# Moving the zero fill of a routed output behind attention, with the last two experts' weights behind the gathers and six output buffers

## The chip, the cores and the metric

One core of a Trainium2 chip. The metric is the device time of one execution in microseconds (us); the kernel before takes 292.96 us, the median of three runs (291.38 to 295.23). The profile was taken in a separate execution, which took 299.41 us and spans 297.6 us from the first to the last instruction. Times read from the profile lie on that longer scale.

## The reference

Two parts follow one another. The first is attention with 32 global and 512 local tokens per head (8 batches, 8 heads, head dimension 64): global queries see all 544 keys; a local query sees the 32 global keys and the local keys within 32 positions of it.

```python
s_g = scale * q_g @ k_all.T                  # k_all = [k_g, k_l]
out_g = sm(s_g) @ v_all
s_ll = where(abs(i - j) <= 32, scale * q_l @ k_l.T, -1e9)
a_l = sm(concat([scale * q_l @ k_g.T, s_ll]))
out_l = a_l @ concat([v_g, v_l])
x = concat([out_g, out_l])                   # rows: 8 * 544 = 4352, columns: 8 * 64 = 512
```

The second is a mixture of 8 experts over the rows of x. Each row goes to the expert with its largest logit; an expert keeps the 80 rows with the largest gate weight; all other rows of the result are zero.

```python
expert_idx = argmax(x @ w_gate); gate_w = softmax(x @ w_gate)[expert_idx]
out = zeros((4352, 512))
for e in range(8):
    tok = rows with expert_idx == e, the 80 with the largest gate_w
    out[tok] = gate_w[tok] * (relu(x[tok] @ w1[e]) @ w2[e])   # w1: 512 x 1024, w2: 1024 x 512
```

So of 4352 rows at most 640 are written with values, and the whole result, 8.9 MB, must first be filled with zeros.

## The kernel before, in words

**Attention** is a loop of 16 steps, q = 0 to 15: batch q // 2, and the heads 0 to 3 or 4 to 7. A step is written out by hand as a sequence of pieces, and pieces of the next steps are laid between those of the current one, so that the order of the program is the order of work on each engine. The pieces that matter here: `load_qk(q + 4)` and `load_v(q + 2)` put the loads of later steps on SyncE's queue; `G_all` (L380) starts the sums of a step on PE with the global keys and needs `vg`; `shift_v` (L209, L210) makes the second, shifted copy of the values on GpSimd and needs the values' loads; `H_chunk` (L393) adds the banded part for a head and divides; `C_chunk` (L436) casts the result on GpSimd into `xb`, of which there are two buffers, one for each of two batches.

**Gating.** `La`, `Lb1`, `Lm`, `Lb2`, `Lb3`, `Lc` compute a batch's logits, the largest one and the gate weights; `Ld` writes the batch's rows to the scratch tensor `x_scr` in HBM by six transfers on SyncE's queue (L541 to L546). They run a batch behind attention. `best` and `rounds` search the 80 largest weights of each expert by repeated 8-fold maxima on DVE, in small pieces (`some`) between the attention's; the last ten rounds, on `fin`, follow when all batches are in (L802).

**Zeros.** `zeros(n)` issues the next n of 17 writes of 512 KB from a zero tile `zt` to the output, on SyncE's queue (L614). The list `NZ` says how many go out in each step: none in q 0 and 1, one in each of q 2 to 13, two in q 14 and three in q 15. `zeros(17)` after the loop (L780) issues what is left.

**Weights.** `load_w(e, parts)` loads an expert's two matrices in four transfers of 512 KB (bf16 on the chip, float32 in HBM; the cast is done by the transfer), on GpSimd's queue: parts 0 and 1 are w1 (L597), parts 2 and 3 are w2 (L601). Experts 0 to 2 (NRES = 3) are loaded one part in each of q 0 to 11. Expert 3 follows in q 12 and 13, expert 4 in q 14 and 15, the first half of expert 5 in q 15, into buffers that attention no longer needs. The rest of expert 5 and all of expert 6 are issued right after attention (L791). Then come two constants, `tri` and `iota1`, also through GpSimd's queue, because they are cast to bf16 (L792, L793).

**Routing.** From the last rounds come the thresholds; `keep` marks the kept rows, `excl` (L822) and the product with `tri` (L825) number them, four one-hot compares with `iota1` (L836) and 40 small products turn the numbers into row indices `idx` (L847). Eight gathers on GpSimd (L851) fetch the experts' rows from `x_scr`. Right behind them stand the four transfers of expert 7 (L854).

**Experts.** A loop over e: `fx(e + 1)` transposes the next expert's rows and copies them (`fxT`, DVE, L864); `fh(e)` multiplies by w1 with a relu on ACT (L872, L874); `fy(e - 1)` multiplies by w2 (L879), scales into `y` on DVE (L882) and scatters y to the output from GpSimd (L885). `y` has three buffers, taken in turn. `warm(n)` issues n products that nobody reads, so that PE does not fall idle.

What sets the order around the change: three queues with an order of their own. SyncE issues loads, zeros and x_scr in program order; GpSimd issues weights, constants, gathers and scatters in program order between its own computing; and DVE runs the rounds, the copies `fxT` and the scaling `y` in program order.

Of the kernel before, what the change touches and what calls it, by code (L numbers as in the profile page):

```python
# [10 lines left out]
FP32 = mybir.dt.float32  # L11
FP16 = mybir.dt.float16
BF16 = mybir.dt.bfloat16
# [10 lines left out]
NRES = 3  # L24
# [62 lines left out]
def kernel(  # L87
# [18 lines left out]
    E = moe_w_gate.shape[1]  # L106
    DF = moe_w1.shape[1]
# [4 lines left out]
    cap = int(moe_capacity)  # L112
# [17 lines left out]
    def psS(shape, dt, name):  # L130
        return ps.tile(shape, dt, tag="S", bufs=2, name=name)
# [4 lines left out]
    def const(name, dt, shape=None):  # L136
        t = cpool.tile(list(shape or c[name].shape), dt, name=name + ("_b" if dt == BF16 else ""))
        eng = nc.sync if dt == mybir.dt.from_np(c[name].dtype) else nc.gpsimd
        eng.dma_start(out=t, in_=cd[name].ap())
        return t  # L140
# [14 lines left out]
    def load_qk(q):  # L155
        b, qd = divmod(q, 2)
        for t, src in ((0, q_l), (1, k_l)):
            hs = src[b, 4 * qd:4 * qd + 4].rearrange("(g a) (p i) d -> (a p) g (i d)", a=2, i=8)
            nc.sync.dma_start(out=qkb[q % 2][:, t].rearrange("p g i d -> p g (i d)"), in_=hs)

    def regroup(q, t):
        if t == 0:
            qkr[q] = lpool.tile([P, 2, 8, 2, D], FP16, tag="qkr", name=f"qkr_{q}")
        nc.scalar.copy(out=qkr[q][:, t].rearrange("p i g d -> p g i d"), in_=qkb[q % 2][:, t])  # L164
# [134 lines left out]
    def kg_copy(q):  # L299
        b, qd = divmod(q, 2)  # L300
        nc.gpsimd.tensor_copy(out=qkT[q % 2][:, :, 512:544], in_=kgp[:, b, 2 * qd:2 * qd + 2, :])

    def kO_copy(q):

        for a in range(2):
            nc.gpsimd.tensor_copy(  # L306
                out=kO[q % 2][:, a],
                in_=qkT[q % 2][:, a, 576:1088].rearrange("x (u w y) -> x u w y", w=2, y=64)[:, :, ::-1, :])
# [285 lines left out]
    def load_w(e, parts):  # L594
        for k in parts:
            if k < 2:
                nc.gpsimd.dma_start(out=w1sb[e][:, 2 * k:2 * k + 2],  # L597
                                    in_=moe_w1[e, 256 * k:256 * k + 256].rearrange("(c p) f -> p c f", p=P))
            else:
                k -= 2  # L600
                nc.gpsimd.dma_start(out=w2sb[e][:, 4 * k:4 * k + 4],  # L601
                                    in_=moe_w2[e, 512 * k:512 * k + 512].rearrange("(p c) f -> p c f", c=4))
# [2 lines left out]
    QB = 1  # L605

    NS = [[1, 1, 1]] * 11 + [[1, 2, 2]] * 4 + [[2, 2, 0]]
    NZ = [0, 0, 1, 1, 1, 1, 1, 1, 1, 1, 1, 1, 1, 1, 2, 3]
    nz = [0]

    def zeros(n):
        for _ in range(n):
            if nz[0] < 17:
                nc.sync.dma_start(out=out_z[nz[0]], in_=zt[:])  # L614
                nz[0] += 1
# [7 lines left out]
    def warm(n):  # L623

        w_ps = psS([P, 512], FP32, "w_ps")
        for _ in range(n):
            nc.tensor.matmul(out=w_ps[:], lhsT=onesb[:], rhs=w1sb[0][:, 0, 0:512], start=True, stop=True)  # L627
# [23 lines left out]
    for q in range(NQ):  # L651
        b, qd = divmod(q, 2)
        first = q == 0
        if 0 < q and q + 4 < NQ:
            load_qk(q + 4)
        if q + 2 < NQ:
            load_v(q + 2)
        zeros(NZ[q])
        if first:
            for t in range(2):  # L660
                regroup(1, t)
            load_qk(3)
        if late is not None:
            Lb3(late)
        G_chunk(q)
        if not first and q + 2 < NQ:
            kg_copy(q + 2)
        G_all(q)
        H_chunk(q, 0)
        Q_chunk(q)  # L670
        if first:
            T_chunk(1, 0)
        elif q + 2 < NQ:
            T_chunk(q + 2, 0)
        if late is not None and q == NQ - 1:
            Lc(late)
            Ld(late)
        if first:
            T_chunk(1, 1)
            kO_copy(1)  # L680
        elif q + 1 < NQ:
            L_fill(q + 1, 0)
            mask(q + 1, 0)
        if pend is not None:
            La(pend)
        if not first and q + 3 < NQ:
            regroup(q + 3, 0)
        if q + 1 < NQ:
            shift_v(q + 1)
        some(NS[q][0])  # L690
        H_chunk(q, 2)
        if pend is not None:
            Lb1(pend)
        some(NS[q][1])
        if first:
            L_fill(1, 0)
            mask(1, 0)
            for t in range(2):
                regroup(2, t)
        else:  # L700
            if q + 1 < NQ:
                L_fill(q + 1, 1)
            if q + 2 < NQ:
                T_chunk(q + 2, 1)
                kO_copy(q + 2)
        H_chunk(q, 1)
        if not first and q + 1 < NQ:
            mask(q + 1, 1)
        if first:
            L_fill(1, 1)  # L710
            mask(1, 1)
            T_chunk(2, 0)
        if late is not None and q < NQ - 1:
            Lc(late)
            Ld(late)
        if q + 1 < NQ:
            G_fill(q + 1)
            Q_fill(q + 1, 0)
        if not first and q + 3 < NQ:
            regroup(q + 3, 1)  # L720
        H_chunk(q, 3)
        if first:
            T_chunk(2, 1)
            kO_copy(2)
        X_chunk(q, 0)
        if q + 1 < NQ:
            Q_fill(q + 1, 1)
        C_chunk(q)
        X_chunk(q, 1)
        if pend is not None:  # L730
            Lm(pend)
            Lb2(pend)
        if q in (1, 3):
            setup_globals(4, 8, 2 - q // 2 - 1)
        if first:
            for t in range(2):
                regroup(3, t)
            load_qk(4)
        some(NS[q][2])
        late = pend  # L740
        pend = b if qd == 1 else None
        st.pop(q)

        if q < 4 * NRES:
            e, k = divmod(q, 4)
            if k == 0:
                w_tiles(e, wpool)
            load_w(e, (k,))
        if q == 12:

            flat = [qkb[i][:].rearrange("p t g i d -> p (t g i d)").bitcast(BF16) for i in range(2)]
            flat += [vb[i][:].rearrange("p s h d -> p (s h d)")[:, 0:2048].bitcast(BF16) for i in (1, 2, 0)]
            for i, f in enumerate(flat):
                if i % 2 == 0:
                    w1sb[NRES + i // 2] = f.rearrange("p (c f) -> p c f", c=4)
                else:
                    w2sb[NRES + i // 2] = f.rearrange("p (c f) -> p c f", c=8)
            load_w(NRES, (0, 1))
        if q == 13:
            load_w(NRES, (2, 3))  # L760
        if q == 14:
            load_w(NRES + 1, (0, 1))
        if q == NQ - 1:
            load_w(NRES + 1, (2, 3))
            load_w(NRES + 2, (0, 1))
    warm(2)
    La(pend)
    warm(3)
# [17 lines left out]
    for e in range(NRES + 2, E):  # L786
        if e > NRES + 2:
            w1sb[e] = w2pool.tile([P, 4, FF], BF16, name=f"w1sb{e}")
        w2sb[e] = w2pool.tile([P, 8, DF], BF16, name=f"w2sb{e}")
        if e < E - 1:  # L790
            load_w(e, (2, 3) if e == NRES + 2 else (0, 1, 2, 3))  # L791
    tri = const("tri", BF16)  # L792
    iota1 = const("iota1", BF16)  # L793
    rpool = ctx.enter_context(tc.tile_pool(name="route", bufs=1, reuse_waits="tile"))
    xg = [rpool.tile([cap, XW], FP32, name=f"xg{e}") for e in range(E)]
    for e in range(E):
# [53 lines left out]
    for e in range(E):  # L850
        nc.gpsimd.indirect_dma_start(out=xg[e][:], out_offset=None, in_=x_dram.ap(),  # L851
                                     in_offset=bass.IndirectOffsetOnAxis(ap=idx[:, e:e + 1], axis=0),
                                     bounds_check=N - 1, oob_is_err=False)
    load_w(E - 1, (0, 1, 2, 3))  # L854
    warm(16)
    xTs, hTs = {}, {}

# [18 lines left out]
    def fy(e):  # L876
        y_ps = psS([cap, DF], FP32, f"y_ps{e}")
        for cc in range(8):
            nc.tensor.matmul(out=y_ps[:], lhsT=hTs[e][:, cc, :], rhs=w2sb[e][:, cc, :],  # L879
                             start=(cc == 0), stop=(cc == 7))  # L880
        y = rpool.tile([cap, DF], FP32, tag="y", bufs=3, name=f"y{e}")
        nc.vector.tensor_scalar(out=y[:], in0=y_ps[:], scalar1=xg[e][:, XW - 1:XW], scalar2=None,  # L882
                                op0=ALU.mult)

        sc = nc.gpsimd.indirect_dma_start(out=out,  # L885
                                     out_offset=bass.IndirectOffsetOnAxis(ap=idx[:, e:e + 1], axis=0),
                                     in_=y[:], in_offset=None, bounds_check=N - 1, oob_is_err=False)
        tc.declare_no_dep(sc.ins, group="scatters", reason="disjoint rows")
        tc.add_to_no_dep_group("scatters", sc.ins)
# [45 lines left out]
```

The softmax here doesn't subtract the row's maximum and nothing guards it: scores larger than these inputs give would overflow.

## Time and profile before

| | |
|---|---|
| device time, median of 3 | 292.96 us |
| span of the profile | 297.6 us |
| busy: PE, DVE, ACT, POOL | 80%, 53%, 46%, 52% |
| DMA: SyncE's queue, GpSimd's queue | 41.44 MB, 18.80 MB; 52.6% and 34.4% of 16 engines |
| 17 zero writes | 512 KB each, 5.1 us from issue to landing (median) |
| first G_all of q 4, of q 15 | 65.15 us, 199.76 us |
| idx ready, first gather issued | 253.3 us, 254.20 us |
| first transfer of expert 7 issued | 264.08 us |

How to read it: PE is TensorE, PEld its weight loads, POOL is GpSimd, SP is SyncE, DVE and ACT are VectorE and ScalarE. A line of the chain of work that ended last gives the start, the duration and what it was, with the line of the code; "DMA a<-b" in it is the time from the issue of a transfer to its landing. A line of the waits gives who waited for whom, the total in us, how often, and the longest. In a table of stretches, the columns are the stretch, its length, then the busy time of PE, PEld, DVE, ACT and POOL with the number of instructions, PE's granted clock, the mean busy share of the 16 DMA engines (it can pass 1, as packets overlap), and the GB/s they moved.

### The profile page before, as it was taken

What the parts mean: (1) busy time and instruction counts of PE and PEld (TensorE: products, weight loads), DVE (VectorE), ACT (ScalarE), POOL (GpSimd) and SP (SyncE); (2) the same over time, 40 slices, a digit from 0 to 9 for tenths busy, and PEclk for the clock granted to TensorE, in tenths of its full rate; (3) what the DMA queues carried; (4) which work ended last, traced back from release to release, by engine and by line L of the source; (5) the groups of instructions that cost most, each with busy time, mean ns of one, the idle gap of its engine ahead of it and who ended that gap; (6) DMA issues with size and microseconds to landing.
All of it is one profiled execution on the core that took longest, in us unless ns stands there. A gap on an engine that the chain in (4) does not pass through costs nothing.

```text
span 297.6 us, 9689 instructions
## 1 busy us (share of the span) xinstructions
PE 238.7 (80%) x4013; PEld 170.2 (57%) x4017; DVE 157.1 (53%) x521; ACT 135.7 (46%) x225; POOL 155.6 (52%) x220
## 2 busy tenths in 40 slices
PE   1377899999969999975999898994969548999490
PEld 1265676876747776854686776673524215477350
DVE  4652344752831466783476469869668836121221
ACT  3376895786772876753469286450100000033010
POOL 2235677683828759642873868764442200682212
PEclk9999999999996999998699799999669975699776
DMA  7899799699999999996999988999999990149411
GB/s 207 217 266 221 258 274 224 127 291 200 239 228 297 245 229 275 201 215 181 263 241 249 280 187 162 262 211 291 219 230 226 223 183 0 46 89 212 120 44 44
DMA packets 70892, 60.86 MB, mean 204 GB/s; under 512 B 49216, under 2 KB 53568, under 8 KB 70848
## 3 DMA queue, kind: packets, MB, share of 16 engines
q1 hardware_dynamic: 63008, 41.44, 52.6%
q0 software_dynamic: 7840, 18.80, 34.4%
q8 instruction: 31, 0.51, 0.7%
q14 instruction: 13, 0.11, 0.1%
HBM read 62.36 MB, written 14.70 MB: 259 GB/s over the span
## 4 chain that ended last, share of the span: by engine, by line
PE 40%; DMA 26%; issue 9%; ACT 8%; DVE 7%; SPq 4%; POOL 4%; POOLq 0%; ACTq 0%; DVEq 0%
PE o_ps L393 7%; DMA tri_b<-ctri 6%; DMA vb<-in_moe_w_dram 5%; PE o_ps L380 5%; DMA x_scr<-xb 4%; PE T_ps L294 4%; DMA vg<-in_v_g_dram 4%; PE og L409 3%; PE x_ps L425 3%; ACT qkT L297 3%; DMA out_dram<-y,idx 3%; DMA vb<-in_q_g_dram 3%; ACT eL L352 2%; PE lt_ps L447 2%; PE l_ps L347 2%
## 5 line engine op out<-in xcount | busy, mean ns | idle before, releaser
L297 ACT COPY qkT<-T_ps 128x1024 f16<-128x1024 f16 x32 | 32.5, 1020 | 46.4 <-PE T_ps L294 42.8
L360 POOL TENSOR_TENSOR eL<-eL,band 128x512 f32<-128x512 f32 x30 | 38.0, 1266 | 20.6 <-ACT eL L352 18.5
L393 PE MATMUL o_ps<-vb,eL 128*64 128x65 f32 x1024 | 45.6, 234 | 0.1
L352 ACT ACTIVATE eL<-l_ps 128x512 f32<-128x512 f32 x64 | 35.0, 603 | 17.6 <-PE l_ps L347 17.6
L398 DVE RECIPROCAL rec<-o_ps 128x4 f32<-128x4 f32 x64 | 11.5, 179 | 58.8 <-PE o_ps L393 58.7
L393 PEld LDWEIGHTS o_ps<-vb,eL 128*64 128x64 f32 x1024 | 36.6, 142 | 10.1 <-issue 5.9
L164 ACT CAST qkr<-qkb 128x1024 f16<-128x1024 f32 x32 | 33.8, 1066 | 3.1 <-DMA qkb<-in_q_l_dram 3.1
L874 ACT ACTIVATE fhT<-h_ps 128x320 bf16<-128x320 f32 x16 | 6.9, 437 | 61.8 <-PE h_ps L872 60.9
L294 PE MATMUL T_ps<-ident,qkr 128*128 128x128 f16 x256 | 22.0, 234 | 9.8 <-ACT qkr L164 8.8
L627 PE MATMUL w_ps<-w1sb,onesb 128*128 128x512 bf16 x87 | 28.7, 488 | 0.5 <-DVE dthr L814 0.2
L399 DVE TENSOR_TENSOR xn<-o_ps,rec 128x256 f32<-128x256 f32 x64 | 27.2, 425 | 3.2
L209 POOL COPY vb<-vb 64x1040 f32<-64x1040 f32 x16 | 16.7, 1042 | 21.4 <-DMA vb<-in_v_l_dram 11.9
L380 PE MATMUL o_ps<-vg,eG 32*128 32x65 f32 x512 | 22.4, 303 | 6.8 <-DMA vg<-in_v_g_dram 6.8
L306 POOL COPY kO<-qkT 128x512 f16<-128x512 f16 x32 | 18.6, 609 | 16.4 <-ACT qkT L297 15.9
L425 PE MATMUL x_ps<-misc,xn 128*128 128x128 f32 x128 | 21.6, 295 | 5.0 <-DVE rec L398 3.3
L380 PEld LDWEIGHTS o_ps<-vg,eG 32*128 32x128 f32 x512 | 20.0, 211 | 9.5 <-DMA vg<-in_v_g_dram 7.6
L294 PEld LDWEIGHTS <-qkr 128*128 128x128 f16 x256 | 16.1, 104 | 12.8 <-ACT qkr L164 9.2
L436 POOL CAST xb<-xn 128x1024 bf16<-128x1024 f32 x16 | 16.6, 1035 | 10.8 <-DMA x_scr<-xb 5.6
L851 POOL DMA_INDIRECT xg<-x_scr,idx x8 | 7.8, 969 | 23.5 <-DVE idx L847 21.4
L627 PEld LDWEIGHTS <-onesb 128*128 128x128 bf16 x91 | 10.3, 119 | 15.8 <-issue 9.9
L425 PEld LDWEIGHTS x_ps<-misc,xn 128*128 128x128 f32 x128 | 14.1, 145 | 7.8 <-issue 3.4
L882 DVE TENSOR_SCALAR y<-y_ps,xg 80x512 f32<-80x512 f32 x8 | 6.0, 746 | 22.8 <-PE y_ps L879 14.6
(142 smaller groups left out, 450.1 us busy)
## 6 DMA issues: line engine op xcount, KB each, us to landing
out_dram<-zt SPq DMA_DIRECT2D x17, 512.0 KB, 5.1
qkb<-in_q_l_dram SPq DMA_DIRECT2D x16, 512.0 KB, 6.5
qkb<-in_k_l_dram SPq DMA_DIRECT2D x16, 512.0 KB, 4.8
vb<-in_v_l_dram SPq DMA_DIRECT2D x48, 128.0 KB, 5.3
w2sb<-in_moe_w_dram POOLq DMA_DIRECT2D x12, 512.0 KB, 9.0
w1sb<-in_moe_w_dram POOLq DMA_DIRECT2D x10, 512.0 KB, 8.4
x_scr<-xb SPq DMA_DIRECT2D x8, 514.0 KB
vb<-in_moe_w_dram POOLq DMA_DIRECT2D x6, 512.0 KB, 15.0
```

What stands on the lines that cost most here:

```text
L164: nc.scalar.copy(out=qkr[q][:, t].rearrange("p i g d -> p g i d"), in_=qkb[q % 2][:, t])
L209: nc.gpsimd.tensor_copy(out=v[0:64, 5:9], in_=v[0:64, 1:5])
L294: nc.tensor.transpose(out=T_ps[:, i].rearrange("x a p -> x (a p)"), in_=qkr[q][:, t, i].rearrange("p g d -> p (g d)"), identity=ident16[:, :])
L297: nc.scalar.copy(out=dst, in_=T_ps[:].rearrange("x i a p -> x a p i"))
L306: nc.gpsimd.tensor_copy(out=kO[q % 2][:, a], in_=qkT[q % 2][:, a, 576:1088].rearrange("x (u w y) -> x u w y", w=2, y=64)[:, :, ::-1, :])
L352: nc.scalar.activation(out=eL[:], in_=l_ps[hh][:], func=AF.Exp, scale=scale)
L360: eng.tensor_tensor(out=eL[:], in0=eL[:], in1=band[:].rearrange("p t i -> p (t i)"), op=ALU.mult)
L380: nc.tensor.matmul(out=s["o"][h][:, u, :], lhsT=s["eG"][32 * r:32 * r + 32, 128 * u:128 * u + 128], rhs=vg[b % 2][32 * r:32 * r + 32, qd, ...
L393: nc.tensor.matmul(out=o[64 * odd:64 * odd + 64, u, :], lhsT=s["eL"][h][:, 64 * t:64 * t + 64], rhs=v[:, 5 * odd + u, h, :], start=False, ...
L399: nc.vector.tensor_tensor(out=s["xn"][:, :, 64 * h:64 * h + 64], in0=o[:, :, 0:64], in1=rec[:].unsqueeze(2).to_broadcast([P, 4, 64]), op=A ...
L425: nc.tensor.transpose(out=x_ps[:, 128 * u:128 * u + 128], in_=s["xn"][:, u, 128 * j:128 * j + 128], identity=identf[:, :])
L627: nc.tensor.matmul(out=w_ps[:], lhsT=onesb[:], rhs=w1sb[0][:, 0, 0:512], start=True, stop=True)
```

## The change

No zeros are written during attention. The first four of the 17 writes stand right behind the attention loop, the other 13 where the remainder stood before, behind `Ld` of the last batch; all of them must have landed before the first scatter. The two constants are loaded in q 14 instead of behind all the weights. The four transfers of expert 6 move from before the routing to behind the gathers, ahead of those of expert 7. `y` gets six buffers. The aim is to keep the zeros' traffic away from the loads that attention waits for, to let the routing wait for no transfer, and to let the results wait for no scatter.

```diff
@@ -605,7 +605,6 @@
     NS = [[1, 1, 1]] * 11 + [[1, 2, 2]] * 4 + [[2, 2, 0]]
-    NZ = [0, 0, 1, 1, 1, 1, 1, 1, 1, 1, 1, 1, 1, 1, 2, 3]
     nz = [0]
@@ -655,7 +654,6 @@
             load_v(q + 2)
-        zeros(NZ[q])
         if first:
@@ -759,10 +757,13 @@
         if q == 14:
+            tri = const("tri", BF16)
+            iota1 = const("iota1", BF16)
             load_w(NRES + 1, (0, 1))
         if q == NQ - 1:
             load_w(NRES + 1, (2, 3))
             load_w(NRES + 2, (0, 1))
+    zeros(4)
     warm(2)
@@ -787,10 +788,7 @@
         w2sb[e] = w2pool.tile([P, 8, DF], BF16, name=f"w2sb{e}")
-        if e < E - 1:
-            load_w(e, (2, 3) if e == NRES + 2 else (0, 1, 2, 3))
-    tri = const("tri", BF16)
-    iota1 = const("iota1", BF16)
+    load_w(NRES + 2, (2, 3))
@@ -851,7 +849,8 @@
-    load_w(E - 1, (0, 1, 2, 3))
+    for e in range(NRES + 3, E):
+        load_w(e, (0, 1, 2, 3))
     warm(16)
@@ -878,7 +877,7 @@
-        y = rpool.tile([cap, DF], FP32, tag="y", bufs=3, name=f"y{e}")
+        y = rpool.tile([cap, DF], FP32, tag="y", bufs=6, name=f"y{e}")
```

## The prediction

> **What bounds the kernel now.** I read the page's slices first, then stretches of the span, the chain that ended last, the waits, and the queues of SyncE and GpSimd around the end. The page's slices (7.44 us each):
>
> ```profile
> PEclk9999999999996999998699799999669975699776
> DMA  7899799699999999996999988999999990149411
> GB/s 207 217 266 221 258 274 224 127 291 200 239 228 297 245 229 275 201 215 181 263 241 249 280 187 162 262 211 291 219 230 226 223 183 0 46 89 212 120 44 44
> ```
>
> The DMA engines are full from slice 2 to slice 32 (15 to 246 us), idle in 33 and 34, full for one slice, then nearly idle. So there are two regimes, and a hole between them. The same in stretches (columns: PE, PEld, DVE, ACT, POOL busy, granted clock, DMA share, GB/s):
>
> ```profile
> 60.00:200.00 140.00, 125.18 (x2495) 95.76 (x2498) 81.75 (x277) 87.29 (x147) 92.46 (x120) 0.94 1.01 235
> 211.00:246.00 35.00, 24.41 (x105) 10.41 (x106) 24.09 (x80) 0.82 (x2) 8.87 (x22) 0.79 1.07 219
> 246.00:265.00 19.00, 18.06 (x176) 10.94 (x178) 6.96 (x13) 1.78 (x5) 8.67 (x10) 0.67 0.15 34
> 265.00:278.00 13.00, 11.40 (x157) 8.07 (x155) 2.12 (x5) 3.36 (x8) 4.61 (x6) 1.00 1.00 199
> ```
>
> In attention PE is also busy, 125 of 140 us. Which one sets the pace shows in the chain, at the start of each q (G_all, L380):
>
> ```profile
> 103.69 1.05 PE o_ps L380 x32
> 113.17 1.16 PE o_ps L380 x31
> 124.93 1.05 PE o_ps L380 x32
> ...
> 133.61 5.70 DMA vg<-in_v_g_dram
> 139.35 2.55 PE o_ps L380 x32
> ```
>
> Undisturbed, two q take 124.93 - 103.69 = 21.2 us. But q 10 starts 14.4 us after q 9, behind a late vg load, and then runs its first stages at half speed (2.55 for 1.05 us). From q 4 (65.15) to q 15 (199.76) eleven q take 134.6 us; at 21.2 a pair they would take 116.8. So late loads cost attention up to 17.8 us.
>
> After attention the chain ends in these waits:
>
> ```profile
> 227.21 19.00 DMA tri_b<-ctri
> 246.25 0.45 PE pos_ps L825
> ...
> 268.47 1.74 PE y_ps L879 x8
> ...
> 271.26 8.55 DMA out_dram<-y,idx
> ```
>
> tri is a 32 KB constant, but queued behind all of e=5 and e=6: it lands 19 us after issue, and the waits charge PE pos_ps 4.4 us to it. Later y3, the first to reuse one of three buffers, waits for a scatter (8.2 us in the waits) that lies in the software queue behind the weights of e=7; behind y3 on DVE stands fxT of e=6, for which PE waits:
>
> ```profile
> DVE y L882 <- DMA out_dram<-y,idx: 8.2, 1, 8.2
> ...
> POOL xb L436 <- DMA x_scr<-xb: 5.6, 1, 5.6
> ...
> PE pos_ps L825 <- DMA tri_b<-ctri: 4.4, 1, 4.4
> ```
>
> **What the Trainium skill says.** "DMA: Bandwidth & Descriptors", section "Issuing engines are not separate DMA queues": what SyncE and GpSimd issue runs on the same 16 DMA engines and interleaves. Agreed: in 60 to 200 us SyncE's queue holds 68.9% and GpSimd's 31.2% of them, together full. So moved zeros only change whom they compete with. Same page, "Queues, rings and completion order": each DMA engine takes turns between queue rows, and starts a ring's descriptors in order. Agreed: tri and the scatter wait behind weights of their own queue, 19 and about 9 us. "TensorE: Matmul & The Clock Gate", "Part 1: The HAM clock gate": an idle window of about 3.4 us halves the clock until some 3.4 us of work. Agreed: after 3.4 us of idle time, 2.55 instead of 1.05 us above, and a granted clock of 0.70 in 140 to 150 us.
>
> **The change, part by part.**
>
> *Zeros out of attention.* The DMA table for 60 to 200 us lists 13 of the 17 writes of 512 KB (0.524 MB); the other four go out by 206. In 200 to 206 us, where they are 90% of the traffic, the queues moved 285 GB/s: 0.524/285 is 1.84 us each. Thirteen make 24 us of full DMA, more than the 17.8 us that loads cost the chain. So attention should become PE's own. I don't take all of it: the loads lag already when q 4 begins (its q and k loads are issued at 74.6, it began at 65.15), before more than two zeros; small disturbances of PE remain. I take two thirds, 12 us; bounds 4 and 17. The 5.6 us wait of xb (GpSimd) is likely to go too, since x_scr of batch 5 (issued 191.00) no longer stands among zeros; it is inside these 12.
>
> *Zeros after attention.* Issue on SyncE takes 0.43 us each. Queued behind the first four there is only Ld(7), six writes to x_scr, which the gathers need some 25 us later: no cost. The other 13 go behind Ld(7): that ends at 227.7 now, so about 216. From about 197 the DMA must move 17 zeros (31 us), e=4's second half and e=5 (six of 0.524 MB at the 196 GB/s of 266 to 276 us: 16 us), and x_scr of two batches (about 3.7 us): 51 us, done at about 248. The scatters wait for the zeros, but are issued after that. No cost, with no slack to the weights behind the gathers.
>
> *tri and iota1 at q 14.* Two issues of 0.53 us on GpSimd. Behind them are e=4's first loads and rv, xgb and xb of q 15; GpSimd sat idle 5.6 us there: nothing. Removed: 4.4 us on the chain, since excl was ready at 242.3 and PE was free.
>
> *DVE's rounds and the rest up to idx* hang on no transfer: from the attention's end they keep their length. So idx, now at 253.3, comes at 253.3 - 12 - 4.4 = 236.9.
>
> *Weights of e=6 and e=7 behind the gathers.* Now e=7 alone is issued at 264.08, 10.8 us after idx (eight gathers of 1.26 us each). Now two experts: eight issues, twice 2.74 us, with the scatters queued behind them on GpSimd; y0 to y5 have buffers, so nobody waits. Data start 1.4 us after issue and run at 196 GB/s, 2.1 MB an expert: 10.7 us each. So e=6 is there at 236.9 + 10.8 + 1.4 + 10.7 = 259.8, and e=7 at 270.5. The experts run 3.03 us apart; e=0 came 6.5 us after idx, so e=6 is due at 236.9 + 6.5 + 18.2 = 261.6: not late. e=7 is due at 264.6; its w1, the first half, is there at 265.2, but fy(7) waits for w2 until 270.5.
>
> *Six buffers.* They take out the 8.2 us wait and the half-speed stage behind it (h 2.29 for 1.31, y 3.55 for 1.90 us). y6 waits for the scatter of y0, which lands just after e=7's weights: under 2 us, beside fy(7). Behind it on DVE stands only y7.
>
> *Sum.* From 270.5: 1 us for the landing to be seen, fy(7) 1.9 to 3.6 us (2.7), and from its last matmul to the end as now 297.6 - 290.7 = 6.9. End at 281.1, against 297.6. The tail from idx keeps its length (44.2, now 44.3): the second expert on the path costs 10.7 and gives back the buffer wait. The gain is 12 + 4.4 us. The profiled execution was a long one; the median is 292.96. 292.96 x 281.1/297.6 is 276.7. Since the median run has likely fewer of the late loads that the change removes, I add 2.3: **279 us**.
>
> **The rivals.**
>
> *Zeros collide with the weights (no change).* For it: 248 us is the very moment at which e=6 starts. If a zero costs 2.4 us (at 219 GB/s, the rate of 211 to 246), 13 from 216 take 31 us, and some 8 more for what the weights of e=5 take: 255. Gathers then land late and e=6, e=7 lose half the engines for about 7 us: with attention giving only 8, the end is near 281.1 + 4 + 4 + 3 = 292, by the ratio 288. Against it: the 285 GB/s seen.
>
> *Attention is not freed (slower).* The lag is SyncE's: its loads, in order, wait for room. If zeros filled gaps only, idx comes at 249, zeros end near 227.7 + 31 + 16 = 275, and take half the engines from e=6 and e=7 for 14 us, 7 lost: e=7 at 289.6. Six scatters of 0.164 MB behind it, 0.84 us each, hold y6 and y7 (5 us), and PE is cold (3 us): 289.6 + 1 + 3.6 + 6.9 + 5 = 306, by the ratio 301. Against it: DMA at 1.01 through 140 us leaves no gaps.
>
> *Everything fits (faster still).* 17 us from attention, fy(7) warm: 275 in the profile, 271.
>
> **How the numbers follow.** Forecast 0.60, everything fits 0.17, collision 0.15, not freed 0.08. Faster by over 2% means under 287.1: the first two, 0.77; within 2% 0.15; slower 0.08. The range runs from 271 to 292: the low end is the best case, the high end takes in the collision with the 4 us bound for attention.
>
> **What would show it.** No zero before the last q; eleven q from 4 to 15 in about 122 us instead of 134.6; no wait on tri; idx near 237; DMA full from 197 to about 248, and again from 250 to 270; y waits on no scatter before y6; y7 behind w2 of e=7. It is wrong if vg or v still comes late at q 6, 10 or 14, or if zeros are still moving when e=6's weights start.

## The result and the profile after

The changed kernel takes 279.16 us (median of 4, 278.71 to 283.38) beside 294.1 us for the kernel before (now four runs): a ratio of 0.952, 95% interval 0.941 to 0.962. The forecast was 279. The first profile of the kernel before shows an execution 5 us longer than its median, so the two spans (297.6 and 277.2 us) differ by more than the times.

The page's slices of the changed kernel, now 6.93 us each:

```profile
PEclk9999999999999999999999999999968967859998
DMA  7998799896979999899899989969999999379981
GB/s 214 236 261 237 210 292 300 174 246 147 257 125 248 201 241 260 173 218 261 165 270 214 235 150 162 198 118 138 273 266 248 273 420 418 103 123 214 216 226 48
```

PE's clock no longer drops anywhere in attention, and the DMA engines now have some free moments there (a share of 0.95 for 1.01); the zeros show as two slices at 420 GB/s (222 to 236 us). In stretches, columns as before:

```profile
60.00:200.00 140.00, 125.92 (x2662) 94.93 (x2661) 95.04 (x329) 89.47 (x151) 99.83 (x133) 1.00 0.95 203
211.00:246.00 35.00, 27.13 (x185) 13.26 (x184) 19.38 (x42) 0.88 (x3) 9.72 (x11) 0.82 0.86 273
246.00:265.00 19.00, 19.00 (x238) 13.20 (x236) 4.88 (x10) 5.02 (x12) 7.91 (x11) 0.88 1.08 208
```

The hole in DMA at 246 to 265 us is filled (1.08 for 0.15): there e=6 and e=7 are loaded. Starts of some q in the chain that ended last:

```profile
86.86 1.05 PE o_ps L380 x32
...
108.04 1.05 PE o_ps L380 x32
119.70 1.05 PE o_ps L380 x32
...
142.64 1.05 PE o_ps L380 x32
```

These are q 6, 8, 9 and 11. Two q take 21.2 us before q 8, and none of these stages runs at half speed. One load is still late: v before q 10, for which GpSimd waits 3.7 us, so that q 9 to q 11 take 22.9 us. From q 4 to q 15 PE now takes 120.3 us, before 134.7. In PE's own timeline the two stages, and the first product with tri, are

```profile
65.24 1.12 PE L380 MATMUL o_ps<-vg,eG 32*128 32x65 f32 x32
...
185.55 1.12 PE L380 MATMUL o_ps<-vg,eG 32*128 32x65 f32 x32
...
226.20 0.47 PE L823 MATMUL pos_ps<-keepx,tri_b 128*128 128x320 bf16 x1
```

The last line has no wait in brackets: the routing no longer waits for tri. idx and the first gather, from the timelines of DVE and GpSimd, of the changed kernel:

```profile
233.10 0.16 DVE L845 TENSOR_TENSOR idx<-idf,inv_ps 80x8 uint32<-80x8 f32 x1
...
234.14 1.04 POOL L849 DMA_INDIRECT xg<-x_scr,idx  x1 [25.84 <-DMA out_dram<-zt]
```

The bracket names a zero as releaser, but it is idx: the gather comes 0.88 us after idx ends, as it did before (253.32 and 254.20). The chain that ended last is led astray in the same way here.

### The profile page after: what moved, and what is told of

The parts are those of the page before. It is cut to its first block, busy times and chain, and to the rows that moved or that the text cites. A ratio compares the mean times of both kernels' runs of the same rounds, so it can differ in the third digit from the quotient of the medians.

```text
span 277.2 us, 9695 instructions
## 1 busy us (share of the span) xinstructions
PE 228.6 (82%) x4017; PEld 161.9 (58%) x4017; DVE 158.6 (57%) x521; ACT 135.7 (49%) x225; POOL 155.0 (56%) x220
## 4 chain that ended last, share of the span: by engine, by line
PE 44%; DMA 17%; ACT 11%; issue 10%; DVE 7%; POOL 6%; SPq 1%; POOLq 1%; ACTq 0%; DVEq 0%
PE o_ps L393 7%; DMA out_dram<-zt 6%; PE x_ps L425 5%; PE T_ps L294 5%; DMA x_scr<-xb 5%; ACT qkT L297 4%; PE o_ps L380 4%; PE y_ps L878 4%; ACT eL L352 3%; PE h_ps L871 3%; PE og L409 3%; DMA vb<-in_v_l_dram 2%; PE lt_ps L447 2%; PE lg L457 2%; PE l_ps L347 2%
## 5 line engine op out<-in xcount | busy, mean ns | idle before, releaser
L393 PE MATMUL o_ps<-vb,eL 128*64 128x65 f32 x1024 | 44.7, 231 | 0.2 <-POOL vb L210 0.2
L352 ACT ACTIVATE eL<-l_ps 128x512 f32<-128x512 f32 x64 | 35.0, 604 | 17.8 <-PE l_ps L347 17.8
L393 PEld LDWEIGHTS o_ps<-vb,eL 128*64 128x64 f32 x1024 | 35.9, 140 | 10.2 <-issue 6.1
L306 POOL COPY kO<-qkT 128x512 f16<-128x512 f16 x32 | 18.6, 608 | 16.5 <-ACT qkT L297 16.0
L626 PE MATMUL w_ps<-w1sb,onesb 128*128 128x512 bf16 x91 | 27.4, 463 | 0.0
L425 PE MATMUL x_ps<-misc,xn 128*128 128x128 f32 x128 | 20.7, 286 | 5.9 <-DVE rec L398 3.4
L209 POOL COPY vb<-vb 64x1040 f32<-64x1040 f32 x16 | 16.7, 1042 | 9.8 <-DMA vb<-in_v_l_dram 9.8
L436 POOL CAST xb<-xn 128x1024 bf16<-128x1024 f32 x16 | 16.5, 1034 | 6.0 <-DVE xn L399 6.0
L380 PE MATMUL o_ps<-vg,eG 32*128 32x65 f32 x512 | 18.8, 285 | 0.0
L425 PEld LDWEIGHTS x_ps<-misc,xn 128*128 128x128 f32 x128 | 13.4, 140 | 8.7 <-issue 3.5
L380 PEld LDWEIGHTS o_ps<-vg,eG 32*128 32x128 f32 x512 | 16.5, 194 | 2.5 <-issue 2.2
L626 PEld LDWEIGHTS <-onesb 128*128 128x128 bf16 x91 | 9.7, 112 | 14.1 <-issue 7.4
L210 POOL COPY vb<-vb 64x1040 f32<-64x1040 f32 x16 | 16.8, 1052 | 0.9
```

The lines of the kernel that those rows point to most:

```text
L210: nc.gpsimd.tensor_copy(out=v[64:128, 5:9], in_=v[64:128, 0:4])
L306: nc.gpsimd.tensor_copy(out=kO[q % 2][:, a], in_=qkT[q % 2][:, a, 576:1088].rearrange("x (u w y) -> x u w y", w=2, y=64)[:, :, ::-1, :])
L352: nc.scalar.activation(out=eL[:], in_=l_ps[hh][:], func=AF.Exp, scale=scale)
L380: nc.tensor.matmul(out=s["o"][h][:, u, :], lhsT=s["eG"][32 * r:32 * r + 32, 128 * u:128 * u + 128], rhs=vg[b % 2][32 * r:32 * r + 32, qd, ...
L393: nc.tensor.matmul(out=o[64 * odd:64 * odd + 64, u, :], lhsT=s["eL"][h][:, 64 * t:64 * t + 64], rhs=v[:, 5 * odd + u, h, :], start=False, ...
L425: nc.tensor.transpose(out=x_ps[:, 128 * u:128 * u + 128], in_=s["xn"][:, u, 128 * j:128 * j + 128], identity=identf[:, :])
```

## The experiments

The edits are printed in short form, without the lines that only follow from them. "The tail" is the stretch from the end of idx to the end of the profile; its length and that of the stretch before it are taken from the profile of each run.

Zeros and the rest, taken apart. **First, the rest alone:** the zeros go back into attention.

```diff
+    NZ = [0, 0, 1, 1, 1, 1, 1, 1, 1, 1, 1, 1, 1, 1, 2, 3]
 ...
+        zeros(NZ[q])
 ...
     zeros(4)                       # stays; finds none left to write
```

> The changed kernel with the zeros back inside attention, one write a step as before; constants, weights and six buffers as changed. My theory: most of the gain is attention that no longer waits for loads, so q 4 to q 15 takes again some 132 to 135 us instead of 120.3, and the time is 289 to 293 us (the kernel before less the wait for tri, 4.4 us, less a little of the tail). Rival: the gain is in the tail (no wait for tri, no wait of y for a scatter), and attention's late loads come from chance; then the time stays within 3 us of the changed kernel, 277 to 282.

Measured: 295.17 us, ratio 1.008 [1.003, 1.014]. q 4 to q 15 took 132.2 us. The rest alone brings nothing; so neither of the two expectations for the time held, though the one for attention did. In its profile (a span of 292.2 us) idx comes at 248.2 us, 5.1 us earlier than in the first profile of the kernel before: 2.5 us less from q 4 to q 15, and 4.3 us less from q 15 to idx, where the wait for tri is gone, but q 4 starts 1.6 us later. The tail keeps 44 us. The medians don't show these 5 us. As that first profile lies 5 us above the median of its kernel, what the end of this wait is worth by itself stays open.

**The zeros alone:** the kernel before with `NZ` removed and `zeros(4)` behind the loop.

```diff
-    NZ = [0, 0, 1, 1, 1, 1, 1, 1, 1, 1, 1, 1, 1, 1, 2, 3]
 ...
-        zeros(NZ[q])
 ...
+    zeros(4)                       # behind the loop; the rest as in the kernel before
```

> The kernel before with nothing changed but the zeros, which stand behind attention. My theory: attention gains its 14 us, but all weights up to e=6 and the zeros now compete before the routing: 26 us of zeros and 27 us of weights from about 195 us end near 248, tri is again the last in its queue and lands near 243 to 248, so idx is as late as before (250 to 255) and the tail keeps its wait for a scatter: 288 to 295 us. Rival: the parts add up, and this one alone brings some 12 us: 280 to 283.

Measured: 289.52 us, ratio 0.982 [0.975, 0.989]. Attention took 119.2 us from q 4 to q 15, 15 us less; only a third arrives at the end. The waits and the chain of this kernel:

```profile
PE pos_ps L824 <- DMA tri_b<-ctri: 10.3, 1, 10.3
```

```profile
212.82 25.43 DMA tri_b<-ctri
238.29 0.45 PE pos_ps L824
```

tri, last in its queue, lands 25 us after its issue. That is 8 us earlier than in the kernel before (238.25 for 246.21), but attention ends 14 us earlier, so the wait grew from 4.4 to 10.3 us, and idx comes at 245.4 us, not between 250 and 255 as expected. So the parts don't add up (0.982 x 1.008 is 0.990, not 0.952): attention's gain passes through only if routing has no transfer to wait for. Less this wait the 289.5 us would be about 279.2, the time of the changed kernel.

**Which part frees tri?** The changed kernel with the constants loaded where they were, behind e=5:

```diff
-            tri, iota1 = const(...)      # in q 14
+    tri, iota1 = const(...)              # behind load_w(NRES + 2, (2, 3))
```

> The changed kernel with tri and iota1 loaded where they were, behind the weights of e=5. Theory one, as predicted: loading them early takes 4.4 us out of the chain, so this gives some of it back, 281 to 284 us. Theory two, after the changed kernel's trace: with e=6 moved behind the gathers GpSimd's queue is empty at about 220 us, and tri is wanted only at 226.5, so the place of tri is worth nothing by itself: 278 to 280.

Measured: 279.5 us, ratio 0.952 [0.944, 0.959], as theory two had it: the place of tri is worth nothing here. With e=6 behind the gathers tri lands in time even as the last in its queue; PE waits for it no more than in the changed kernel.

**e=6 back before the routing**, constants early:

```diff
     load_w(NRES + 2, (2, 3))
+    load_w(NRES + 3, (0, 1, 2, 3))       # and only e=7 behind the gathers
```

> The changed kernel with the weights of e=6 issued before the routing, as they were; only e=7 follows the gathers. My theory: these 10.7 us of DMA fit ahead of the routing, because the zeros moved at 1.3 us each, not 1.84; zeros end near 247 instead of 238 and slow the gathers and the first part of e=7, but e=7 lands some 5 to 8 us earlier (near 260), and then PE is the last: 4 to 7 us less, 272 to 275. Rival: the zeros and gathers get in each other's way, e=7 lands as late as now: 279 to 284.

Measured: 277.01 us, ratio 0.937 [0.926, 0.948]. At least as good as the changed kernel; the intervals overlap. The time lies between the two expectations. The tail is 40.7 us long, for 43.9 in the changed kernel, although the first rows are used only 6.5 us after their gather is issued. Nobody waits for tri here either: either move frees it, both are not needed.

**Three buffers for y** in the changed kernel:

```diff
-        y = rpool.tile(..., tag="y", bufs=6)
+        y = rpool.tile(..., tag="y", bufs=3)
```

> The changed kernel with three buffers for y. My theory: y3, due at 259.6 us, must wait for the scatter of y0, which lies behind the weights of e=7 and lands near 268; the copy for e=6 stands behind y3 on DVE, PE stops after fy(3) or fy(4) for some 6 us and runs e=6 and e=7 afterwards partly at half speed: 6 to 9 us more, 285 to 288. Rival: the tail is bound by the landing of e=7's weights in any case, and the buffers are worth 1 to 2 us: 280 to 281.

Measured: 289.68 us, ratio 0.985 [0.978, 0.993]; more than expected. The wait, which was 8.2 us in the kernel before, when one expert stood ahead of the scatters, is now for two:

```profile
DVE y L881 <- DMA out_dram<-y,idx: 19.3, 1, 19.3
```

**Eight buffers:** the same line with `bufs=8`.

> The changed kernel with eight buffers for y, so that no y waits for a scatter. My theory: y6 no longer waits for the scatter of y0 (2.8 us in the changed kernel, 9.6 us where PE was quicker), but y7 waits for fy(7), which waits for e=7's w2, so the end moves by 1 us or less: 277.5 to 279.5. Rival: the wait of y6 is what sets the end; 2 us less or more.

Measured: 282.47 us, ratio 0.952 [0.940, 0.963], the ratio of six buffers; the tail has 44.3 us. y6 now waits for fy(6), which stands on PE behind the h of e=7 and so waits for e=7's w1. The scatter ahead of y6 set nothing that shows.

**No zeros at all:** `if nz[0] < 0` in `zeros`, so nothing is written but the scatters.

> The changed kernel with no zero written at all (so rows that no expert keeps stay unwritten). What do the zeros still cost where they stand now? My theory: idx comes from DVE's rounds, the first gather follows idx by 0.9 us as before, and the zeros are through at about 238 us; only the gathers land sooner (4.2 us after issue now, 2.6 without): first gather at 233 to 234.5 us, time 277 to 279.5. Rival: the zeros hold the gathers, as the waits name them for 25.8 us before the first gather; then the gathers go out earlier and the time falls by 4 us or more, below 275.

Measured: 281.93 us (277.74 to 285.34), ratio 0.961 [0.949, 0.974]: above what was expected, and no faster than with zeros. The same two lines as above:

```profile
231.78 0.16 DVE L845 TENSOR_TENSOR idx<-idf,inv_ps 80x8 uint32<-80x8 f32 x1
...
232.81 1.04 POOL L849 DMA_INDIRECT xg<-x_scr,idx  x1 [26.18 <-DVE idx L845]
```

0.87 us again, and now idx is named: the zeros did not hold back the issue of the gathers. Where they stand in the changed kernel, the zeros cost nothing that these runs show.

**What makes zeros hurt?** The kernel of zeros_in_attention, with the zeros issued from another engine: first ScalarE, then GpSimd.

```diff
-                nc.sync.dma_start(out=out_z[nz[0]], in_=zt[:])
+                nc.scalar.dma_start(out=out_z[nz[0]], in_=zt[:])    # second: nc.gpsimd
```

> As zeros_in_attention (zeros inside attention, the rest as changed), but the zeros are issued from ScalarE's queue instead of SyncE's, so no load stands behind a zero in a queue's order. What makes zeros hurt attention? My theory: the time of the 16 DMA engines, which both queues share; then q 4 to q 15 still takes 128 to 135 us and the time stays at 289 to 297. Rival: the order in SyncE's queue, where each load waits for the zero ahead of it; then attention takes 120 to 123 us and the time is 279 to 284.

Measured: 292.69 us; in its profile 135.4 us from q 4 to q 15. But 9.7 of these are one wait, in which ScalarE itself stood still until it had issued a zero (88.79 us), while the profile names the landing of a load of values, so this run decides nothing.

> As zeros_in_attention, but the zeros are issued from GpSimd's queue, where they share a ring with the weights, which nobody in attention waits for. From ScalarE's queue the test was spoilt: one issue held ScalarE itself for 9.7 us. Theory one: what loads lose to zeros is total time of the 16 DMA engines; then it does not matter which queue the zeros take, q 4 to q 15 takes 128 to 135 us, and the time is 289 to 296. Theory two: loads lose only what stands in their own queue ahead of them, and a share of the engines against other queues that does not grow when those have more work; then attention takes 120 to 124 us, the weights come later instead, and the time is 276 to 283.

Measured: 299.74 us, ratio 1.027 [1.017, 1.038]; 136.7 us from q 4 to q 15, both somewhat above theory one, and some 4.5 us more than with the zeros on SyncE's queue. GpSimd was not held as ScalarE had been: each of these issues took 0.5 to 0.6 us. The loads are as late as ever:

```profile
POOL vb L209 <- DMA vb<-in_v_l_dram: 15.1, 4, 6.9
...
PE o_ps L380 <- DMA vg<-in_v_g_dram: 7.8, 4, 4.0
```

In the chain of work the late stages stand behind loads that took long, though no zero stood ahead of them in SyncE's queue:

```profile
84.50 7.29 DMA vg<-in_v_g_dram
...
91.84 2.69 PE o_ps L380 x32
...
111.16 6.34 DMA vg<-in_v_g_dram
```

The longest transfer of vg took 9.4 us from issue to landing here and 8.4 with the zeros on SyncE's queue, but 5.6 in the changed kernel and in zeros_alone. And this is what the engines moved meanwhile, by the DMA table: the kernel before from 65 to 199 us, the changed one from 65 to 185, and zeros from GpSimd from 66 to 200 us.

```profile
DMA packets 40137, 31.25 MB, mean 233 GB/s; under 512 B 29168, under 2 KB 31892, under 8 KB 40113
```

```profile
DMA packets 36549, 24.57 MB, mean 205 GB/s; under 512 B 27180, under 2 KB 30001, under 8 KB 36525
```

```profile
DMA packets 40409, 30.99 MB, mean 231 GB/s; under 512 B 29230, under 2 KB 32302, under 8 KB 40386
```

With zeros in attention, 31 MB go in 134 us, with the engines' busy share at 1.01 and 1.00, whichever of the two queues the zeros are in. Without them 24.6 MB go in 120 us, at 0.95. So it is the time of the DMA engines that counts, not the order in SyncE's queue. Whether the engines or the memory behind them set the rate, these runs don't tell.

**The kernel before once more**, for a second profile:

> The kernel before once more, for a second profile: the first was of an execution 5 us longer than the median. My theory: its idx and tri stand near 249 us instead of 253, because the DMA engines, full from 15 us on, set when tri lands, and a shorter execution has fewer late loads and a longer wait for tri; the tail from idx stays 44 us. Rival: the late loads are the same, and the 5 us lie in the tail.

Measured: 294.59 us (two executions), but the profiled one was again long (297.69), so the question of a shorter one is not answered. It repeats attention (132.9 us), idx (252.25) and the tail (43.6 us); the wait for tri was 2.4 us.

**Two versions that go on from here.** `best` (the name of the run, not the search of the gating) takes e=6 before the routing, eight buffers, and six of the zeros at the end of q 13, where SyncE has no more loads:

```diff
         if q == 13:
+            zeros(6)
             load_w(NRES, (2, 3))
```

> The changed kernel with e=6 before the routing, eight buffers, and six of the zeros issued at the end of q 13, behind the last values' loads, where SyncE has nothing more to load and the DMA share falls to 0.44. My theory: zeros are through near 236 us again, gathers are undisturbed, e=7 lands near 256, before its turn at 261, so PE sets the tail: end near 270 us in the profile, time 270 to 273. Rival: zeros in q 14 and 15 delay attention again (later loads are done, but casts of x_scr and weights are not): 275 to 280.

Measured: 275.25 us, ratio 0.938 [0.928, 0.948], more than the 270 to 273 expected. The time is the rival's, but not for its reason: attention keeps its pace (118.6 us). The first expert starts late:

```profile
233.97 1.03 POOL L851 DMA_INDIRECT xg<-x_scr,idx  x1 [22.13 <-DMA out_dram<-zt]
...
240.60 0.45 PE L862 MATMUL xT_ps<-identbf,xg 80*128 80x80 bf16 x4 [2.19 <-DMA xg<-x_scr,idx]
```

6.6 us from the issue of a gather to the use of its rows. In `best_half` only w1 of e=6 goes ahead:

```diff
-    load_w(NRES + 3, (0, 1, 2, 3))
+    load_w(NRES + 3, (0, 1))             # (2, 3) behind the gathers
```

> As best, but only w1 of e=6 is issued before the routing; its w2 goes behind the gathers, ahead of e=7. My theory: in best the gathers stand in GpSimd's queue behind the last of e=6's weights (first gather issued at 233.97 us, its rows used at 240.6, 6.6 us later; 3.7 without zeros); with half of e=6 gone from before them they land by 238, and e=7, due at 259 to 261, lands near 261: 2 to 3 us less than best, 272 to 273.5. Rival: what delays the gathers is the zeros beside them, not the weights ahead: then no gain, or 1 us lost to e=7's later landing, 275 to 277.

Measured: 275.68 us (274.3 to 277.65, 6 runs), no less than `best`, so the expected 272 to 273.5 was missed. In the profile the tail does get shorter, 38.1 us for 40.5 in `best`: the first rows are used 3.7 us after the issue of their gather, although the last four products of e=7 now wait 1.6 us for w2. But idx itself came 3.6 us later (236.7 for 233.1), and 2.7 of these lie in attention (121.3 for 118.6 us), which the edit doesn't touch; why stays open.

What had held the rows in `best` is not settled by this. There, from 236 to 238 us, GpSimd's queue had 1% of the DMA engines and the zeros 99%, and the rows landed when the zeros ran out at about 240 us. Here the zeros were nearly through when the first gather went out at 237.6 us. So the zeros beside the gathers explain it as well as the weights ahead of them. Both versions lie some 3 to 4 us below the changed kernel in the medians; the interval of `best` overlaps that of the changed kernel, and for `best_half` none is on record.

## Why the prediction was right

*The hit itself.* That 279.16 us fell on 279 is in part luck. The working ended at 281.1 us on the scale of the profile, and the profile ends at 277.2: the sum was 3.9 us too high, 2.2 from attention, 1.4 between q 15 and idx, 0.3 from the tail. On that scale the gain was 20.4 us, not 16.5. Between the medians it is 14.9 us, as the profile before was of a long execution. The forecast's step from the one scale to the other, by the ratio of the spans and 2.3 us of judgement, took off 2.5 us (16.5 to 14) where the runs show 5.5. So two errors of 3 to 4 us cancelled.

*Attention, 12 of 17.8 us.* 14.4 us, within the bounds of 4 and 17. The mechanism is shown: 6.7 MB less for the DMA engines, no half-speed stage, late loads gone but for small ones, and the 14 us come back when the zeros do, from SyncE's queue and from GpSimd's. One sign of being wrong did appear, in small: v comes late before q 10, at 3.7 us.

*The zeros' size.* 1.84 us each was too much. When they have the engines to themselves (225 to 235 us of the changed kernel) the DMA table says

```profile
DMA packets 1150, 4.19 MB, mean 419 GB/s; under 512 B 128, under 2 KB 128, under 8 KB 1149
```

that is 0.524/419, or 1.25 us. In the 285 GB/s of the prediction other traffic was mixed in. So they were through by about 237 us, not 248, and the collision could not come.

*tri, 4.4 us.* On the profile's scale the size was near: from q 15 to idx the changed kernel takes 47.7 us, before 53.6, and zeros_in_attention 49.3. But the early load, to which the prediction put it down, is only one of two moves that each suffice: with e=6 behind the gathers it adds nothing (tri_late). And the size was no constant: 2.4 us in one profile of the kernel before, 4.4 in the other, 10.3 where only the zeros had moved. The last is what tri behind all the weights costs once attention is faster.

*idx at 236.9.* It came at 233.3: 2.2 us from attention and 1.4 between q 15 and idx. No run took the latter apart; in the ten profiles other than the changed kernel's in which PE doesn't wait for tri, this stretch takes 47.7 to 49.3 us, so that it may be no more than spread.

*The tail, 44.2 us from idx.* 43.9. How it arises is shown best by tri_late, from PE's timeline, for e=7:

```profile
259.50 0.26 PE L871 MATMUL h_ps<-fxT,w1sb 128*128 128x80 bf16 x2 [1.60 <-DMA w1sb<-in_moe_w_dram]
261.98 2.19 PE L871 MATMUL h_ps<-fxT,w1sb 128*128 128x80 bf16 x30 [2.21 <-DMA w1sb<-in_moe_w_dram]
263.96 5.27 PE L878 MATMUL y_ps<-w2sb,fhT 128*80 128x512 bf16 x16
```

h of e=7 waits for w1, then fy(6) and fy(7) follow, in 5.27 us instead of some 3.6. So the second expert behind the gathers does set the end, as worked out, but through another half of its weights: the prediction had w1 there in time and fy(7) waiting for w2, while here no wait for w2 is named. In the changed kernel itself not even this wait is seen: PE got there later, for another reason (below), and found e=7's weights there. That its tail has the predicted length is therefore in part luck; the two tails, 43.9 and 43.8 us, agree.

*Six buffers.* In place of the predicted 8.2 us wait, three would have cost 19.3 us of waiting and about 10 us of time, because two experts now stand ahead of the scatters. y6's wait, put under 2 us, was 2.8 us here and 9.6 in tri_late; eight buffers bring no time that shows.

*The rivals.* Collision and "not freed" are excluded by no_zeros and by attention's 120.3 us. Not foreseen was that the zeros alone would bring only 1.8% and the rest alone nothing: the prediction added parts that in truth need one another.

## What to carry to other kernels

A bulk write that nobody waits for still costs, if the DMA engines are full and something else waits for a transfer: put it where no transfer beside it is waited for. Another queue did not help here. When a stage gets faster, ask which transfer the next stage waits for, since the gain may turn into a longer wait there (4.4 to 10.3 us here). A releaser that a wait names should be held against the time since the other candidate: 0.88 us behind idx with zeros and 0.87 without them settled it.

## What the runs showed of the hardware

- In the changed kernel, and in no other profile of this study, PE paused in the middle of e=1, with nothing named:

```profile
241.17 0.34 PE L871 MATMUL h_ps<-fxT,w1sb 128*128 128x80 bf16 x4 [0.50 <-issue]
...
242.59 0.33 PE L871 MATMUL h_ps<-fxT,w1sb 128*128 128x80 bf16 x4 [1.08 <-issue]
...
244.01 0.42 PE L871 MATMUL h_ps<-fxT,w1sb 128*128 128x80 bf16 x4 [1.09 <-issue]
```

  Four products, then 1.1 us of nothing, for some 5 us in all; the cause is open. The tail is no longer for it than in tri_late (43.9 and 43.8 us), where PE, without the pause, waits for the weights of e=7.
- The rate at full DMA engines differs with the traffic: 419 GB/s for zeros alone, 233 in the attention of the kernel before, where 29168 of 40137 packets are under 512 B, 196 to 215 for the weights.
- With zeros issued by ScalarE, that engine's own work once stood still for 9.7 us, until a zero had been issued.
